# Top-k attention with a hard-swish feed-forward: the mask as a steep parametric ReLU on ScalarE, normalisation on GpSimd, and a lag of two steps

## The chip, the core and the metric

The kernel runs on one core of a Trainium2 chip. The metric is the device time of one execution in microseconds (us); the median of the runs is what is compared. The engines are TensorE (PE in the profile, its weight loads PEld), VectorE (DVE), ScalarE (ACT), GpSimd (POOL) and SyncE (SP), which issues the DMAs. Each works through its own queue in order.

## The reference

All tensors are fp32 for the kernel's computing; the two feed-forward weights arrive as 64-bit floats. For 8 batches and 8 heads, with 576 positions and a head size of 64:

```python
scores = (1.0 / np.sqrt(D)) * np.matmul(q, k.transpose(0, 1, 3, 2))
kth = np.partition(scores, -32, axis=-1)[..., -32:-31]     # 32nd largest of each row
scores = np.where(scores >= kth, scores, -1e9)
scores = scores - scores.max(-1, keepdims=True)
attn = np.exp(scores)
attn = attn / (attn.sum(-1, keepdims=True) + 1e-9)
x = np.matmul(attn, v)                  # then (B, H, S, D) -> (B*S, H*D) = (4608, 512)
h = x @ w_in                            # w_in (512, 2048)
out = (h * np.clip(h + 3.0, 0.0, 6.0) / 6.0) @ w_out       # w_out (2048, 512)
```

## The kernel before

Heads are taken in pairs (four per batch), and the 576 query rows of a pair are cut into four blocks of 128 and a rest of 64. A *unit* is one block of one pair: a full unit has 128 query rows of two heads, so 1152 scores in each partition; a rest unit has 64 rows of each head, one head in each half of the partitions, 576 scores in each partition. A batch has 20 units in five groups of four full units and one rest unit (rest last in even batches, first in odd ones): 160 units in all.

What a unit goes through:

- `scores` (L213, rest L206): TensorE multiplies into the PSUM tile `big`. `big` has one buffer, which scores, transposes of weights and transposes of inputs take in turn. ScalarE copies it to the SBUF tile `sc` (L214 and L217, rest L208).
- `top(0)` to `top(3)` (L230, L234): VectorE takes eight maxima of each row at a time and replaces them in a work tile `wk`, four times, until `m` holds the 32 largest.
- `mask` (L244, L249, L252): GpSimd compares each score with the 32nd maximum and writes 0 or -3e38 into `wk`, adds that to `sc`, and multiplies the row's maximum by minus the scale (`shift`).
- `exp` (L257): ScalarE computes exp(scale * score + shift) in place, with the row's sum in `den`; GpSimd adds 1e-9 (L262).
- `weights` (L266, L268): VectorE takes the reciprocal of `den`, ScalarE multiplies each row with it.
- `transpose` (L279, L281): TensorE transposes `sc` by blocks of 128 into `big` (nine blocks, six for a rest unit), ScalarE copies them to `eT`.
- `values` (L291, L411): TensorE multiplies with v into the PSUM tile `pv`, for two full units together or for one rest unit; ScalarE copies to `xT` or `xr`.

When four pairs of a block are there, a feed-forward is appended to a list `todo`. `piece` takes the next part from it: eight halves of an `h` tile (eight products of 128x128 each, L310; after each second one ScalarE's Relu, L318, and two pieces later VectorE's gate, L322), then eight parts of `acc` (L329), and at the end ScalarE's output copy (L339) and a DMA.

The tiles `f`, `h`, `pv` and `acc` share four PSUM buffers. In the first steps the 32 chunks of the feed-forward weights are converted from 64-bit to 32-bit by ScalarE (L106, L109), GpSimd (L107, L120) and VectorE (L115, L116); `convert_step` ends one chunk and begins another.

The order on every engine is the order in which the main loop issues the work (`manual_schedule`). A step n of this loop issues: scores of unit n+1; normalisation of unit d; `top(0)` of unit n; two pieces; `top(1)`; transposes of unit d; `top(2)`; a piece; transposes of the next pair's inputs, where due; a piece; values of unit d; `top(3)`; in every fourth step two more pieces; exp of unit n-1; mask of unit n. Here d = n - LAG with LAG = 3. In the first eight steps d = n - 1, and exp, normalisation, transposes and values of unit n-1 all stand in step n; steps 8 and 9 have no transposes.

Of the kernel before, what the change touches and what calls it, by code (L numbers as in the profile page):

```python
# [8 lines left out]
AF = mybir.ActivationFunctionType  # L9
ALU = mybir.AluOpType  # L10
F32 = mybir.dt.float32
# [3 lines left out]

TOP_K = 32
LOWEST = -3.4028234663852886e38
DROP = -3.0e38
EPS = 1.0e-9


# [5 lines left out]
def kernel(  # L27
# [9 lines left out]
    nc = tc.nc  # L37
    P = nc.NUM_PARTITIONS
    B, H, S, D = q.shape
# [8 lines left out]
    scale = 1.0 / float(D) ** 0.5  # L48

    def pool(name, bufs, **kw):  # L50
        return ctx.enter_context(tc.tile_pool(name=name, bufs=bufs, **kw))
# [1 line left out]
    consts = pool("consts", 1)  # L53
    ldpool = pool("ld", 2)
    kqpool = pool("kq", 2 * NHP)
    scpool = pool("sc", 5)
    wkpool = pool("wk", 2)
    mpool = pool("m", 4)
    etpool = pool("et", 2)
# [34 lines left out]
    def convert(dst, src):  # L94

        st = kqpool.tile([P, 2 * WC], U32, tag="kq", name="st")
        nc.sync.dma_start(st[:], src)  # L100
        words = st[:].rearrange("p (n two) -> p n two", two=2)
        lo, hi = words[:, :, 0], words[:, :, 1]
        a = gpool.tile([P, WC], F32, tag="g", name="a")
        y = gpool.tile([P, WC], F32, tag="g", name="y")
        f = ps_w.tile([P, WC], F32, tag="w", name="f")
        nc.scalar.activation(a[:], hi.bitcast(F32), AF.Abs)  # L106
        nc.gpsimd.tensor_scalar(a[:], a[:], HI_MOST, HI_LEAST, ALU.min, ALU.max)  # L107

        nc.scalar.activation(f[:], lo, AF.Copy, bias=2.0, scale=2.0**-51)  # L109
        yield  # L110

        au, yu = a[:].bitcast(U32), y[:].bitcast(U32)
        nc.vector.tensor_scalar(au, au, 3, None, ALU.logical_shift_left)  # L115
        nc.vector.scalar_tensor_tensor(  # L116
            out=yu, in0=hi, scalar=0x80000000, in1=f[:].bitcast(U32),
            op0=ALU.bitwise_and, op1=ALU.bitwise_or,
        )
        nc.gpsimd.tensor_tensor(  # L120
            dst.bitcast(I32), a[:].bitcast(I32), y[:].bitcast(I32), ALU.add
        )
# [63 lines left out]
    class Unit:  # L186
# [49 lines left out]
                    )  # L236
                    self.cur[t] = wk

        def mask(self):

            nt = self.nt
            self.shift = mpool.tile([P, 2], F32, tag="shift", name="shift")
            for t in range(nt):
                nc.gpsimd.tensor_scalar(  # L244
                    self.wk[:, t, :], self.row[t], self.m[:, t, TOP_K - 1 : TOP_K], DROP,
                    ALU.is_lt, ALU.mult,
                )
            both = self.sc[:, 0 : nt * S]
            nc.gpsimd.tensor_tensor(  # L249
                both, both, self.wk[:, 0:nt, :].rearrange("p t s -> p (t s)"), ALU.add  # L250
            )
            nc.gpsimd.tensor_scalar_mul(self.shift[:, 0:nt], self.m[:, 0:nt, 0], -scale)  # L252

        def exp(self):
            self.den = mpool.tile([P, 2], F32, tag="den", name="den")
            for t in range(self.nt):
                nc.scalar.activation(  # L257
                    self.row[t], self.row[t], AF.Exp, bias=self.shift[:, t : t + 1],
                    scale=scale, accum_out=self.den[:, t : t + 1],
                )  # L260
            d = self.den[:, 0 : self.nt]
            nc.gpsimd.tensor_scalar_add(d, d, EPS)  # L262

        def weights(self):
            d = self.den[:, 0 : self.nt]
            nc.vector.reciprocal(d, d)  # L266
            for t in range(self.nt):
                nc.scalar.activation(  # L268
                    self.row[t], self.row[t], AF.Copy, scale=self.den[:, t : t + 1]
                )  # L270

        def transpose(self):
# [10 lines left out]
        def values(self, dst):  # L283
            pr, eT = self.pair, self.eT
            for c in range(J + 1):
                for hh in range(2):
                    if self.rest:
                        rhs = eT[:, c if c < J else J + hh, hh * R : (hh + 1) * R]
                    else:
                        rhs = eT[:, c if hh == 0 or c == J else J + 1 + c, :]  # L290
                    nc.tensor.matmul(  # L291
                        dst[hh * D : (hh + 1) * D, :],
                        pr.vm[:, hh, c, :] if c < J else pr.vr[:, hh, :],
                        rhs,
                        start=(c == 0),
                        stop=(c == J),
                    )
# [51 lines left out]
    units = []  # L349
# [7 lines left out]
    NU = len(units)  # L357
# [3 lines left out]
    def piece(count=1):  # L361
        for _ in range(count):
            while todo:
                try:
                    gates.append(next(todo[0]))
                    break
                except StopIteration:
                    todo.pop(0)
            else:
                gates.append(None)  # L370
            if len(gates) > 2:
                gate = gates.pop(0)
                if gate:
                    gate()
# [4 lines left out]
    def convert_step(depth=1):  # L379

        if converting and (len(converting) > depth or not chunks):
            next(converting.pop(0), None)
        if chunks:
            c = convert(*chunks.pop(0))
            next(c)
            converting.append(c)

    EARLY = 8
    LAG = 3
    state = {}  # L390

    def values(n):
# [30 lines left out]
    def pair_at(n, first):  # L423

        b, at = divmod(n, per_batch)
        hp, odd = divmod(at - first, 3)
        return pairs[b + 1, hp] if b + 1 < B and not odd and 0 <= hp < NHP else None
# [12 lines left out]

    for n in range(NU + LAG):
        early = n < EARLY
        u = units[n] if n < NU else None
        full = not (u and u.rest)
        d = n - (1 if early else LAG)
        d = d if 0 <= d < NU and (early or d >= EARLY - 1) else None
        depth = 2 if n < 3 else 1
        if n + 1 < NU:
            units[n + 1].scores()
        if n < 2:  # L450
            pairs[0, n + 2].transpose()
        if n == 0:
            pairs[0, 3].load()
        if n in (1, 2):
            pairs[0, n + 1].load_values()
        if d is not None and not early:
            units[d].weights()
        if u:
            u.begin()
            u.top(0)  # L460
        p = pair_at(n, 6)
        if p:
            p.load()
            p.load_values()
        convert_step(depth)
        piece(2 if full else 1)
        if u:
            u.top(1)
        if d is not None:
            if early:  # L470
                units[d].exp()
            else:
                units[d].transpose()
        convert_step(depth)
        if u:
            u.top(2)
        piece()
        convert_step(depth)
        if d is not None and early:
            units[d].weights()  # L480
            units[d].transpose()
            piece()
        p = pair_at(n, 8)
        if p:
            p.transpose()
        if full and not early:
            piece()
        if d is not None:
            values(d)
        if u:  # L490
            u.top(3)
        convert_step(depth)
        if n % 4 == 3 and n > 2 * EARLY:
            piece(2)
        if not early and 1 <= n < NU + 1:
            units[n - 1].exp()
        if u:
            u.mask()
    while todo:
        piece()  # L500
    piece(2)
# [34 lines left out]
```

## Time and profile before

| | |
|---|---|
| median of three runs | 1865.07 us (1863.63 to 1865.53) |
| the profiled execution | 1863.41 us |
| its span in the profile | 1861.6 us |
| mean granted TensorE clock | 0.95 |
| busy: TensorE, VectorE, GpSimd, ScalarE | 90%, 83%, 62%, 52% of the span |

Busy times are sums over the whole span, which has three parts. In the first 200 us or so the weights are converted and TensorE is often idle. Then comes a long middle, in which the same pattern of work repeats every two batches (40 units), about 430 us. At the end, from about 1785 us, VectorE is done and TensorE works off what is left of the feed-forward. In the timeline a line gives start, duration, engine, line, operation and tiles; in brackets stands the idle time just before it and what ended that. In the list of waits the numbers are the total in us, the count and the longest. In the table of stretches, each engine's busy time stands with its count of instructions in the order TensorE, its weight loads, VectorE, ScalarE, GpSimd; the granted clock, the DMA share and GB/s follow.

### The profile page before, as it was taken

The numbers are of one execution on the slowest core, as the hardware profiler recorded it, in microseconds if no ns is written. First come the engines' busy times: TensorE is split into PE (matmuls) and PEld (weight loads), VectorE is DVE, ScalarE is ACT, GpSimd is POOL, SyncE is SP. The second block draws the span as 40 slices with busy tenths as digits, with TensorE's granted clock in tenths as the row PEclk, the third lists the DMA queues.
The fourth block names the chain that finished last, engine by engine and source line by source line (L and its number), as shares of the span: only waits on it lengthen the run. The fifth ranks groups of instructions, "written<-read, shape, count | busy, mean of one in ns | idle before, by whom it ended". The sixth has DMA issues, their size and how long they took to land.

```text
span 1861.6 us, 31024 instructions
## 1 busy us (share of the span) xinstructions
PE 1671.3 (90%) x11872; PEld 1217.5 (65%) x11872; DVE 1549.7 (83%) x3249; ACT 969.4 (52%) x1717; POOL 1157.0 (62%) x878
## 2 busy tenths in 40 slices
PE   3346799899999999899999999989999999989999
PEld 2244676567777776577677776667677767666685
DVE  5777998899988888989999888989898888989930
ACT  4553555465555555555555555555555555555540
POOL 4875676566676666666666556666666666667630
PEclk9878799899999999899999999989999999989999
DMA  6341100101001100101001100011001100000000
GB/s 190 124 122 42 43 7 7 44 20 26 7 7 45 50 7 7 45 1 45 7 6 26 45 26 7 18 34 45 7 7 26 45 26 7 6 7 7 7 7 12
DMA packets 101141, 56.54 MB, mean 30 GB/s; under 512 B 84096, under 2 KB 92288, under 8 KB 100992
## 3 DMA queue, kind: packets, MB, share of 16 engines
q1 hardware_dynamic: 100992, 54.55, 10.7%
q8 instruction: 94, 1.54, 0.4%
q14 instruction: 55, 0.45, 0.1%
HBM read 45.09 MB, written 9.44 MB: 29 GB/s over the span
## 4 chain that ended last, share of the span: by engine, by line
PE 83%; ACT 7%; POOL 6%; issue 2%; SPq 1%; DVE 1%; DMA 0%; ACTq 0%; POOLq 0%
PE h L310 28%; PE acc L329 25%; PE pv L291 10%; PE big L279 9%; PE big L213 7%; POOL wk L244 3%; POOL sc L249 2%; PE big L206 2%; ACT sc L257 2%; PE big L178 2%; ACT eT L281 2%; ACT sc L214 1%; ACT sc L268 1%; ACT a L106 1%; DMA st<-in_moe_w_in_dram 0%
## 5 line engine op out<-in xcount | busy, mean ns | idle before, releaser
L244 POOL TENSOR_SCALAR wk<-sc,m 128x576 f32<-128x576 f32 x288 | 637.1, 2220 | 14.4
L230 DVE MAX8 m<-wk 128x8 f32<-128x576 f32 x864 | 619.3, 759 | 2.8
L329 PE MATMUL acc<-w_out,g 128*128 128x512 f32 x1152 | 531.0, 601 | 0.3 <-DVE g L322 0.3
L310 PE MATMUL h<-xT,w_in 128*128 128x128 f32 x4096 | 491.6, 278 | 12.5 <-DVE y L116 10.7
L310 PEld LDWEIGHTS h<-xT,w_in 128*128 128x128 f32 x4096 | 471.6, 193 | 19.4 <-DVE y L116 11.1
L234 DVE MATCH_REPLACE8 wk<-m,wk 128x576 f32<-128x576 f32 x576 | 426.9, 754 | 0.0
L249 POOL TENSOR_TENSOR sc<-sc,wk 128x1152 f32<-128x1152 f32 (+1 forms) x160 | 381.9, 2387 | 13.4
L262 POOL TENSOR_SCALAR den<-den 128x2 f32<-128x2 f32 (+1 forms) x160 | 35.6, 223 | 547.1 <-ACT sc L257 522.6
L329 PEld LDWEIGHTS acc<-w_out,g 128*128 128x128 f32 x1152 | 206.3, 190 | 204.7 <-issue 199.7
L279 PE MATMUL big<-ident,sc 128*128 128x128 f32 x1344 | 198.4, 292 | 117.3 <-ACT sc L268 91.3
L279 PEld LDWEIGHTS big<-ident,sc 128*128 128x128 f32 x1344 | 163.6, 150 | 169.9 <-issue 109.8
L257 ACT ACTIVATE sc<-sc,shift 128x576 f32<-128x576 f32 x288 | 220.6, 769 | 50.2 <-POOL shift L252 49.8
L281 ACT COPY eT<-big 128x1152 f32<-128x1152 f32 (+1 forms) x160 | 168.8, 1055 | 135.4 <-PE big L279 134.9
L318 ACT ACTIVATE g<-h,three 128x512 f32<-128x512 f32 x144 | 99.0, 687 | 247.0 <-PE h L310 247.0
L230 DVE MAX8 m<-sc 128x8 f32<-128x576 f32 x288 | 205.0, 753 | 20.5 <-ACT sc L217 20.5
L234 DVE MATCH_REPLACE8 wk<-m,sc 128x576 f32<-128x576 f32 x288 | 213.0, 750 | 0.0
L268 ACT ACTIVATE sc<-sc,den 128x576 f32<-128x576 f32 x288 | 210.4, 777 | 2.6 <-DVE den L266 2.6
L291 PE MATMUL pv<-eT,vm 128*64 128x128 f32 (+1 forms) x2560 | 178.5, 287 | 19.3 <-ACT eT L281 19.3
L213 PE MATMUL big<-kq 64*128 64x512 f32 (+1 forms) x1024 | 178.7, 470 | 17.1 <-ACT eT L281 8.7
L291 PEld LDWEIGHTS pv<-eT,vm 128*64 128x64 f32 x2560 | 148.1, 150 | 58.1 <-ACT eT L281 38.7
L322 DVE SCALAR_TENSOR_TENSOR g<-g,h 128x512 f32<-128x512 f32 x144 | 99.0, 687 | 102.4 <-ACT g L318 102.4
L213 PEld LDWEIGHTS big<-kq 64*128 64x128 f32 x1024 | 93.9, 198 | 132.9 <-issue 96.6
(42 smaller groups left out, 999.6 us busy)
## 6 DMA issues: line engine op xcount, KB each, us to landing
kin<-in_k_dram SPq DMA_DIRECT2D x64, 128.0 KB, 2.9
qin<-in_q_dram SPq DMA_DIRECT2D x64, 128.0 KB, 2.9
st<-in_moe_w_in_dram SPq DMA_DIRECT2D x16, 512.0 KB, 4.4
vm<-in_v_dram SPq DMA_DIRECT2D x64, 128.0 KB, 2.4
st<-in_moe_w_out_dram SPq DMA_DIRECT2D x16, 512.0 KB, 3.7
out_dram<-o SPq DMA_DIRECT2D x32, 256.0 KB, 2.3
rest<-in_k_dram SPq DMA_DIRECT2D x32, 32.0 KB, 2.5
rest<-in_q_dram SPq DMA_DIRECT2D x32, 32.0 KB, 2.6
```

Source lines behind the costliest of these rows:

```text
L213: nc.tensor.matmul(banks[:, 2 * i + hh, 0 : s1 - s0], pr.qT[d, qs], pr.kT[d, s0:s1])
L230: nc.vector.max(self.m[:, t, 8 * r : 8 * r + 8], self.cur[t])
L234: nc.vector.match_replace(wk, self.m[:, t, 8 * r : 8 * r + 8], self.cur[t], LOWEST)
L244: nc.gpsimd.tensor_scalar(self.wk[:, t, :], self.row[t], self.m[:, t, TOP_K - 1 : TOP_K], DROP, ALU.is_lt, ALU.mult,)
L249: nc.gpsimd.tensor_tensor(both, both, self.wk[:, 0:nt, :].rearrange("p t s -> p (t s)"), ALU.add)
L257: nc.scalar.activation(self.row[t], self.row[t], AF.Exp, bias=self.shift[:, t : t + 1], scale=scale, accum_out=self.den[:, t : t + 1],)
L268: nc.scalar.activation(self.row[t], self.row[t], AF.Copy, scale=self.den[:, t : t + 1])
L279: nc.tensor.transpose(ps[:, i * P : (i + 1) * P], self.sc[:, c0 : c0 + P], ident[:])
L281: nc.scalar.copy(eT[:, 0:n, :].rearrange("p c q -> p (c q)"), ps[:, 0 : n * P])
L291: nc.tensor.matmul(dst[hh * D : (hh + 1) * D, :], pr.vm[:, hh, c, :] if c < J else pr.vr[:, hh, :], rhs, start=(c == 0), stop=(c == J),)
L310: nc.tensor.matmul(h[:, (f - f0) * P : (f - f0 + 1) * P], w_in[:, i, f * P : (f + 1) * P], xT[:, i, :], start=(i == 0), stop=(i == NHP - 1),)
L329: nc.tensor.matmul(acc[:], gs[f // 4][:, (f % 4) * P : (f % 4 + 1) * P], w_out[:, f, :], start=(f == 0), stop=(f == NFC - 1),)
```

## The change

`mask` is gone. In its place `exp` issues three small GpSimd operations (minus the 32nd maximum as `kth`; the scaled difference of the 32nd and the first maximum as `shift`), then on ScalarE for each row of the unit a parametric ReLU of score + kth with the slope 2^120 below zero, and then exp. What is below the threshold becomes hugely negative, and its exp zero; what is kept is the difference from the threshold, which the shift makes up for. Normalisation moves from ScalarE (a copy with a scale) to GpSimd (a multiplication by the reciprocal and by 1). `exp` of unit n stands at the end of step n, where mask stood, and normalisation of unit n-1 in step n after `top(2)` and a piece; both for all steps. LAG is 2, so step 8 alone has no transposes, and `sc` has four buffers instead of five.

```diff
-DROP = -3.0e38
+STEEP = 2.0**120
...
-    scpool = pool("sc", 5)
+    scpool = pool("sc", 4)
...
-        def mask(self):
+        def exp(self):
             nt = self.nt
-            self.shift = mpool.tile([P, 2], F32, tag="shift", name="shift")
+            kth = mpool.tile([P, 2], F32, tag="kth", name="kth")
+            shift = mpool.tile([P, 2], F32, tag="shift", name="shift")
+            self.den = mpool.tile([P, 2], F32, tag="den", name="den")
+            last = self.m[:, 0:nt, TOP_K - 1]
+            nc.gpsimd.tensor_scalar_mul(kth[:, 0:nt], last, -1.0)
+            nc.gpsimd.tensor_tensor(shift[:, 0:nt], last, self.m[:, 0:nt, 0], ALU.subtract)
+            nc.gpsimd.tensor_scalar_mul(shift[:, 0:nt], shift[:, 0:nt], scale)
             for t in range(nt):
-                nc.gpsimd.tensor_scalar(
-                    self.wk[:, t, :], self.row[t], self.m[:, t, TOP_K - 1 : TOP_K], DROP,
-                    ALU.is_lt, ALU.mult,
-                )
-            both = self.sc[:, 0 : nt * S]
-            nc.gpsimd.tensor_tensor(
-                both, both, self.wk[:, 0:nt, :].rearrange("p t s -> p (t s)"), ALU.add
-            )
-            nc.gpsimd.tensor_scalar_mul(self.shift[:, 0:nt], self.m[:, 0:nt, 0], -scale)
-        def exp(self):
...
+                nc.scalar.activation(
+                    self.row[t], self.row[t], AF.Prelu, bias=kth[:, t : t + 1], scale=1.0,
+                    alpha=STEEP,
+                )
+            for t in range(nt):
                 nc.scalar.activation(
-                    self.row[t], self.row[t], AF.Exp, bias=self.shift[:, t : t + 1],
-                    scale=scale, accum_out=self.den[:, t : t + 1],
+                    self.row[t], self.row[t], AF.Exp, bias=shift[:, t : t + 1], scale=scale,
+                    accum_out=self.den[:, t : t + 1],
                 )
...
         def weights(self):
             d = self.den[:, 0 : self.nt]
             nc.vector.reciprocal(d, d)
             for t in range(self.nt):
-                nc.scalar.activation(
-                    self.row[t], self.row[t], AF.Copy, scale=self.den[:, t : t + 1]
+                nc.gpsimd.tensor_scalar(
+                    self.row[t], self.row[t], self.den[:, t : t + 1], 1.0, ALU.mult, ALU.mult
                 )
...
-    LAG = 3
+    LAG = 2
...
-        if d is not None and not early:
-            units[d].weights()
         if u:
             u.begin()
             u.top(0)
...
         if d is not None:
-            if early:
-                units[d].exp()
-            else:
+            if not early:
                 units[d].transpose()
...
+        if 1 <= n < NU + 1:
+            units[n - 1].weights()
         if d is not None and early:
-            units[d].weights()
             units[d].transpose()
             piece()
...
-        if not early and 1 <= n < NU + 1:
-            units[n - 1].exp()
         if u:
-            u.mask()
+            u.exp()
```

More of the change, by code (lines that the diff above doesn't have):

```diff
@@ L237, in top @@
                     self.cur[t] = wk
-        def mask(self):
+        def exp(self):
             nt = self.nt
-            self.shift = mpool.tile([P, 2], F32, tag="shift", name="shift")
+            kth = mpool.tile([P, 2], F32, tag="kth", name="kth")
[5 more added lines that the diff above has]
+            nc.gpsimd.tensor_scalar_mul(shift[:, 0:nt], shift[:, 0:nt], scale)
             for t in range(nt):
-                nc.gpsimd.tensor_scalar(
-                    self.wk[:, t, :], self.row[t], self.m[:, t, TOP_K - 1 : TOP_K], DROP,
-                    ALU.is_lt, ALU.mult,
-                )
-            both = self.sc[:, 0 : nt * S]
-            nc.gpsimd.tensor_tensor(
-                both, both, self.wk[:, 0:nt, :].rearrange("p t s -> p (t s)"), ALU.add
-            )
-            nc.gpsimd.tensor_scalar_mul(self.shift[:, 0:nt], self.m[:, 0:nt, 0], -scale)
-        def exp(self):
-            self.den = mpool.tile([P, 2], F32, tag="den", name="den")
-            for t in range(self.nt):
+                nc.scalar.activation(
+                    self.row[t], self.row[t], AF.Prelu, bias=kth[:, t : t + 1], scale=1.0,
+                    alpha=STEEP,
+                )
+            for t in range(nt):
                 nc.scalar.activation(
-                    self.row[t], self.row[t], AF.Exp, bias=self.shift[:, t : t + 1],
-                    scale=scale, accum_out=self.den[:, t : t + 1],
+                    self.row[t], self.row[t], AF.Exp, bias=shift[:, t : t + 1], scale=scale,
+                    accum_out=self.den[:, t : t + 1],
                 )
-            d = self.den[:, 0 : self.nt]
+            d = self.den[:, 0:nt]
             nc.gpsimd.tensor_scalar_add(d, d, EPS)
```

## The prediction

> **What bounds the kernel now.** I began with the page: busy times and the chain that ended last.
>
> ```profile
> PE 1671.3 (90%) x11872; PEld 1217.5 (65%) x11872; DVE 1549.7 (83%) x3249; ACT 969.4 (52%) x1717; POOL 1157.0 (62%) x878
> PE 83%; ACT 7%; POOL 6%; issue 2%; SPq 1%; DVE 1%; DMA 0%; ACTq 0%; POOLq 0%
> ```
>
> TensorE carries the chain, so I asked where it isn't busy. The stretches of the span give two answers. In the first 200 us it is busy for 91 us; from 200 to 1780 for 1502 of 1580 us. The list of waits from 210 to 1780 us, TensorE alone, is short:
>
> ```profile
> PE big L279 <- ACT sc L268: 34.8, 16, 2.6
> PE pv L291 <- ACT eT L281: 16.9, 14, 1.2
> PE big L279 <- issue: 14.3, 19, 0.9
> ```
>
> L279 are the nine transposes of a unit's weights. They need the single PSUM tile `big`, thus the copy of the next scores out of it, and the normalised weights (L268). None of TensorE's waits names the mask (L244, L249). POOL's mask does hold VectorE (104.7 us at L234 from 230 to 1780), but VectorE has that time to spare there. So in the long middle the mask's 1000 us of POOL are covered; there it counts what ScalarE does between two steps of TensorE. The timeline of one step shows the race:
>
> ```profile
> 598.31 1.30 PE L213 MATMUL big<-kq 64*128 64x512 f32 x8
> 598.91 0.77 ACT L257 ACTIVATE sc<-sc,shift 128x576 f32<-128x576 f32 x1
> 599.53 2.05 PE L310 MATMUL h<-xT,w_in 128*128 128x128 f32 x16
> 600.42 0.99 ACT L214 COPY sc<-big 128x1024 f32<-128x1024 f32 x1
> 601.47 1.45 ACT L268 ACTIVATE sc<-sc,den 128x576 f32<-128x576 f32 x2
> 602.36 1.38 PE L279 MATMUL big<-ident,sc 128*128 128x128 f32 x9 [0.77 <-issue]
> ```
>
> TensorE does scores and one feed-forward piece and is there 3.28 us after 598.31; ScalarE does exp, copy and the first product and is ready after 4.05. With two pieces TensorE comes after 5.07 and waits for nothing; with none it waits 2 to 2.6 us.
>
> At the start the mask is on the path. From one reciprocal to the next:
>
> ```profile
> 62.56 0.17 DVE L266 RECIPROCAL den<-den 128x2 f32<-128x2 f32 x1 [1.77 <-POOL den L262]
> 73.31 0.61 POOL L107 TENSOR_SCALAR a<-a 128x512 f32<-128x512 f32 x1 [5.63 <-ACT a L106]
> 73.91 4.66 POOL L244 TENSOR_SCALAR wk<-sc,m 128x576 f32<-128x576 f32 x2
> 81.62 0.78 ACT L257 ACTIVATE sc<-sc,shift 128x576 f32<-128x576 f32 x1 [6.21 <-POOL shift L252]
> 83.94 0.17 DVE L266 RECIPROCAL den<-den 128x2 f32<-128x2 f32 x1 [7.49 <-POOL den L262]
> ```
>
> **Part 1, the start (mask off POOL, products on POOL).** Out of the loop go the mask, 4.66 + 2.61 + 0.24 with gaps 7.4 us, and ScalarE's first product, 0.8. In come three small POOL operations at 0.23 (row L252), 0.7; two Prelus, for which I take L268's pair, 0.67 from start to start, 1.3; the first product on POOL; and a queue. `exp` now stands at the end of a step, so POOL's `den` stands ahead of three chunks of weight conversion, and the products stand behind those. The third clamp (L107) needs ScalarE to have done the scores' copy (1.2) and three pairs L106/L109 (1.2 each): 5.5 us after `den` the products start. The product's price is the large unknown; POOL has no such multiplication in this trace. Nearest rows:
>
> ```profile
> L107 POOL TENSOR_SCALAR a<-a 128x512 f32<-128x512 f32 x32 | 20.2, 633 | 44.1 <-ACT a L106 43.6
> L244 POOL TENSOR_SCALAR wk<-sc,m 128x576 f32<-128x576 f32 x288 | 637.1, 2220 | 14.4
> ```
>
> Both do two operations on one input. L107 scaled to 576 columns gives 0.71 us; L244, with a pointer scalar as in the change but a comparison, 2.22. I take 0.71, because two plain arithmetic operations are L107's form, and keep 2.22 for the range. The Trainium skill (GPSIMD Engine Reference, 3.1) says that a body of at most two operations runs at 1.03 cycles an element, and that data-dependent branching costs about 12; by that estimate the product is about 0.5 us plus dispatch and the start would gain some 2 us more, while L244 with 2220 ns shows that it isn't so for every two-operation form.
>
> Per loop: -7.4 - 0.8 + 0.7 + 1.3 + 0.7 + 5.5 = 0. The loops alone give nothing, and what is gained lies elsewhere. The first exp no longer waits for the first mask (43.4 us now; small operations after the clamp at 35.1, so 36.7): -6.7. The three stalls of 3.6, 4.1 and 6.4 us in which VectorE's L116 waits for POOL behind a mask (at 113, 130 and 150 us) shorten; POOL is blocked by `den` instead, so I count half, -7. Between the early steps and the late ones the order has two steps without transposes now (lag 3), one after (lag 2), and the transposes of unit 7 at 192.7 wait 8.9 us behind the next unit's exp, which waits for its mask; that goes, but copies and scores that were in the gap then take time: -4. Against it, TensorE reaches the feed-forward with one scores (1.3) and one pair transpose (1.5) not yet done: +2.8. Sum -15. Bounds: 0 (POOL product 2.22 in each of some eight loops) to -30 (the stalls go entirely and the gap too).
>
> **Part 2, the middle.** ScalarE's sum per unit is the same: two products (1.45) go, two Prelus come. But their place changes. The products stood behind the scores' copy and only the first had to be done; both Prelus stand ahead of the copy, and the transposes wait for its end. From the start of `exp`: now 1.51 (exp) + 1.05 (copy) + 0.78 + 0.11 = 3.45; after, 1.34 + 1.51 + 1.17 + 0.11 = 4.13. So +0.68 us per full unit wherever TensorE is already waiting. Lag 2 also changes which step the values (L291) end in. From the order of the built instructions, over the repeating 40 units (430 us): of the steps between scores and transposes four have no piece now and five after; seven have one piece now, six after, and in five of these the values come just before, so that the copy L411 (0.39 with its latency) stands ahead of the Prelus.
>
> One piece: ready after 0.39 + 4.13 = 4.52 against 3.25, idle 1.27 (four times), 1.48 behind the output copy, 0.9 where the next unit is a rest unit (its copy is 0.63): 7.5 us. Now the trace has 0.67, 0.93, 0.77, 0.86, 0.50, 0.50: 4.2. No piece: now 2.55 and three times 2.05, 8.7; after 3.2, 1.4 (exp of a rest unit, 1.6, ends before the scores do) and three times 2.2: 11.2. Copies L281 with nothing beside them: five now, six after, at 1.21: 6.1 and 7.3. Together 19.0 and 26.0 us: +7 per 430 us. Three whole rounds and the last 20 units (+5): +26.
>
> The clock adds to it. The step with no piece at 844.9 us (idle 2.05, then 1.21 before the values) shows in the stretches as
>
> ```profile
> 840.00:850.00 10.00, 6.74 (x45) 4.51 (x45) 10.00 (x24) 6.06 (x10) 6.72 (x4) 0.82 0.45 114
> 850.00:860.00 10.00, 10.00 (x84) 8.85 (x81) 9.82 (x21) 5.18 (x10) 6.56 (x6) 0.84 0.39 93
> ```
>
> PEclk is the third number from the end: (0.18 + 0.16) x 10 = 3.4 us lost, 0.9 of it idle already counted: 2.5 for the new step of this kind, four times, +10. The Trainium skill (TensorE: Matmul & The Clock Gate, HAM oscillation) names idle gaps over about 3.4 us as what throttles; by it neither gap would cost clock and the middle would be +26. The row shows 2.05 and 1.21 us enough, so I keep +36.
>
> What is hidden: VectorE's reciprocal moves behind `top(2)`; behind it stand gates and `top(3)`. It waits for `den`, 3.4 us after ScalarE starts `exp`; VectorE then has 1.4 us to its step's end, and TensorE's step takes 7 to 14, so VectorE stays ahead (five units take it 47 us, from 197.3 to 246.9 less a stall of 2.5, and TensorE 54, an eighth of 430). If that lead went, ScalarE's Prelu would wait for VectorE's last maximum, with scores' copy, Relus and TensorE's transposes queued behind: up to 2 us in each step with no piece, 40 us in all. POOL after: three small operations, two products, `den`, 2.5 us per unit; nobody waits for that in the middle. A fourth buffer of `sc` suffices: the row is transposed two steps later. SP's queue and the DMAs are in the same order, one step apart at most.
>
> **Sum.** The profiled execution took 1863.4 (span 1861.6); the median shown is 1.7 above it. 1863.4 - 15 + 36 = 1884.4, with the 1.7 about 1886. The case's own range, with clock from 0 to +15 and the start from -25 to -5: 1866 to 1902.
>
> **Rivals.** A, faster: the start alone counts. If the transposes in steps with one and no piece wait no longer than now, the middle stays and the time is 1850. It decides at the 0.68 us between products behind and Prelus ahead of the copy: for it, ScalarE is 52% busy and before the copy often idle for 2 to 3 us, in which a Prelu could run early; against it, the 598 us timeline, in which ScalarE has no gap. B: POOL's product costs 2.22, the start gains nothing: 1863.4 + 36 + 1.7 = 1901. Against it L107. C: the idle of 1.3 to 1.5 us in the one-piece steps throttles the clock too, 6 x 3.6 times 1.7 us (the loss at 470 us): +37, 1923. Against it, 0.9 us now costs nothing (clock 1.00 around 602); the threshold lies between 0.9 and 3.3. D: start and middle cancel, 1865. That Prelu lies in another table than Exp and ScalarE reloads all the time: the built order has one table load, as now, so I give it nothing.
>
> **Numbers.** My case 0.50, A 0.22, B 0.13, C 0.07, D 0.08. The range 1848 to 1912 leaves out C and the lower half of A. About 0.2% (4 us) is what a measurement can tell from no change. Faster 0.22, same 0.08, slower 0.70.
>
> **What would show it.** Right: Prelu near 0.77 us, POOL's product near 0.7; TensorE's waits at the transposes name the scores' copy (L215, L218), 1.2 to 1.5 us in steps with one piece; the first piece of the second feed-forward near 195 us instead of 210.5; clock dips at five places per round. Wrong: Prelu's wait for POOL or VectorE in every step (VectorE leads less than I think), products of 2 us, or total TensorE idle after 230 us at or under today's 75 us.

## The result and the profile after

The changed kernel took 1877.74 us (median of four runs, 1876.84 to 1879.55) against 1865.30 of the kernel before beside it (1863.63 to 1865.76). The ratio is 1.007, 95% interval 1.0052 to 1.0087: slower by 0.7%, where 1886 was forecast. The profiled execution took 1877.58 us, its span grew from 1861.6 to 1875.8. Some line numbers shift: Prelu is L251, exp L256, `den` L261, the reciprocal L265, the product L267, the transposes L278, the copy of `eT` L280, the copies of the scores L215 and L218.

Busy times and the chain that ended last, from the page of the changed kernel:

```profile
PE 1672.3 (89%) x11872; PEld 1228.7 (66%) x11872; DVE 1550.3 (83%) x3249; ACT 964.2 (51%) x1717; POOL 409.0 (22%) x1038
PE 82%; ACT 10%; issue 3%; POOL 3%; DVE 1%; SPq 1%; DMA 1%; ACTq 0%
```

GpSimd lost two thirds of its work (1157.0 to 409.0 us) and the kernel became slower. ScalarE does as much as before, and its share of the chain rose from 7 to 10%. The costs of the new operations, from the costliest groups with shapes apart (busy time and mean ns of one behind the first bar):

```profile
L267 POOL TENSOR_SCALAR sc<-sc,den 128x576 f32<-128x576 f32 x288 | 212.5, 747 | 368.3 <-DVE den L265 362.9 <-PE big L278 2.4 <-PE h L309 1.6
L251 ACT ACTIVATE sc<-sc,kth 128x576 f32<-128x576 f32 x288 | 208.7, 769 | 34.3 <-POOL kth L247 34.3
L247 POOL TENSOR_SCALAR kth<-m 128x2 f32<-128x2 f32 x128 | 29.1, 227 | 89.2 <-DVE m L231 88.8
```

All three are near the forecast (0.71, 0.77 and 0.23 us). TensorE's waits in the middle, from 210 to 1790 us (total, count, longest):

```profile
PE big L278 <- ACT sc L218: 44.4, 20, 3.2
PE big L278 <- POOL den L261: 23.4, 18, 1.4
PE pv L290 <- ACT eT L280: 21.7, 18, 1.2
PE big L214 <- ACT kq L185: 5.1, 4, 1.3
PE big L278 <- ACT sc L209: 3.7, 4, 0.9
```

The first two and the last are the transposes, 34.8 + 14.3 us before and 71.5 after (L209 is the scores' copy of a rest unit). The second names POOL's `den`, but misleadingly, as one step in the timeline shows:

```profile
599.63 1.30 PE L214 MATMUL big<-kq 64*128 64x512 f32 x8
599.75 0.37 ACT L410 COPY xT<-pv 128x256 f32<-128x256 f32 x1 [1.66 <-PE pv L290]
600.01 1.44 ACT L251 ACTIVATE sc<-sc,kth 128x576 f32<-128x576 f32 x2
...
600.86 2.05 PE L309 MATMUL h<-xT,w_in 128*128 128x128 f32 x16
601.36 0.76 ACT L256 ACTIVATE sc<-sc,shift 128x576 f32<-128x576 f32 x1
...
602.12 0.76 ACT L256 ACTIVATE sc<-sc,shift 128x576 f32<-128x576 f32 x1
...
602.87 0.99 ACT L215 COPY sc<-big 128x1024 f32<-128x1024 f32 x1
603.05 0.22 POOL L261 TENSOR_SCALAR den<-den 128x2 f32<-128x2 f32 x1 [7.68 <-ACT sc L256]
...
603.76 0.27 ACT L218 COPY sc<-big 128x128 f32<-128x128 f32 x1
...
604.13 1.18 PE L278 MATMUL big<-ident,sc 128*128 128x128 f32 x9 [1.22 <-POOL den L261]
```

`den` was done at 603.27; what ended at 604.03, just before the transposes, is the second half of the scores' copy, on ScalarE. The queue there is copy of `xT`, two Prelus, two exps, copy: ready 4.50 us after the scores began, where TensorE came after 3.28. The row that the prediction worked out as 4.52 is this one.

At the start, one loop:

```profile
55.14 0.28 POOL L247 TENSOR_SCALAR kth<-m 128x2 f32<-128x2 f32 x1
...
55.45 1.44 ACT L251 ACTIVATE sc<-sc,kth 128x576 f32<-128x576 f32 x2 [0.56 <-POOL kth L247]
...
58.48 0.22 POOL L261 TENSOR_SCALAR den<-den 128x2 f32<-128x2 f32 x1 [2.61 <-ACT sc L256]
58.78 1.39 POOL L121 TENSOR_TENSOR w_in<-a,y 128x512 int32<-128x512 int32 x1
...
64.06 0.61 POOL L108 TENSOR_SCALAR a<-a 128x512 f32<-128x512 f32 x1
...
64.77 1.47 POOL L267 TENSOR_SCALAR sc<-sc,den 128x576 f32<-128x576 f32 x2
...
65.57 2.18 PE L278 MATMUL big<-ident,sc 128*128 128x128 f32 x9 [9.33 <-POOL sc L267]
```

The exp chain begins 4.9 us earlier than in the loop before (55.45 for 60.32), but between `den` and the products POOL works off three additions (L121) and three clamps (L108) of the conversion: the products start 6.3 us after `den`.

**Ledger of the span.** Since the order repeats, the transposes of one unit in each 40 serve as a mark; in the kernel before they stand at 359.86 and 1649.94 us, after at 346.81 and 1663.03, three rounds apart. The first piece of the second feed-forward came at 191.97 instead of 210.51 (-18.5), with 2.5 us of other work not yet done: start -16. From there to the first mark +3; three rounds of 438.7 instead of 430.0, +26; the rest +1. Sum +14.

### The profile page after: what moved, and what is told of

Read it like the earlier page. It is cut to its first block, busy times and chain, and to the rows that moved or that the text cites. A ratio compares the mean times of both kernels' runs of the same rounds, so it can differ in the third digit from the quotient of the medians.

```text
span 1875.8 us, 30943 instructions
## 1 busy us (share of the span) xinstructions
PE 1672.3 (89%) x11872; PEld 1228.7 (66%) x11872; DVE 1550.3 (83%) x3249; ACT 964.2 (51%) x1717; POOL 409.0 (22%) x1038
## 4 chain that ended last, share of the span: by engine, by line
PE 82%; ACT 10%; issue 3%; POOL 3%; DVE 1%; SPq 1%; DMA 1%; ACTq 0%
PE h L309 27%; PE acc L328 25%; PE pv L290 11%; PE big L278 9%; PE big L214 6%; ACT sc L256 3%; ACT eT L280 2%; ACT sc L251 2%; PE big L207 2%; PE big L179 2%; ACT sc L215 1%; POOL a L108 1%; POOL w_in L121 1%; ACT o L338 1%; POOL w_out L121 1%
## 5 line engine op out<-in xcount | busy, mean ns | idle before, releaser
L278 PE MATMUL big<-ident,sc 128*128 128x128 f32 x1344 | 189.8, 289 | 122.5 <-ACT sc L218 49.2
L267 POOL TENSOR_SCALAR sc<-sc,den 128x576 f32<-128x576 f32 x288 | 212.5, 747 | 368.3 <-DVE den L265 362.9
L278 PEld LDWEIGHTS big<-ident,sc 128*128 128x128 f32 x1344 | 163.2, 150 | 163.5 <-POOL den L261 78.4
L280 ACT COPY eT<-big 128x1152 f32<-128x1152 f32 (+1 forms) x160 | 169.1, 1057 | 183.3 <-PE big L278 183.3
L251 ACT ACTIVATE sc<-sc,kth 128x576 f32<-128x576 f32 x288 | 208.7, 769 | 34.3 <-POOL kth L247 34.3
L261 POOL TENSOR_SCALAR den<-den 128x2 f32<-128x2 f32 (+1 forms) x160 | 34.9, 218 | 868.1 <-ACT sc L256 868.1
L256 ACT ACTIVATE sc<-sc,shift 128x576 f32<-128x576 f32 x288 | 219.4, 763 | 3.3 <-ACT sc L251 0.4
L290 PE MATMUL pv<-eT,vm 128*64 128x128 f32 (+1 forms) x2560 | 188.6, 298 | 25.4 <-ACT eT L280 25.4
L290 PEld LDWEIGHTS pv<-eT,vm 128*64 128x64 f32 x2560 | 157.1, 156 | 62.9 <-ACT eT L280 32.0
L214 PE MATMUL big<-kq 64*128 64x512 f32 (+1 forms) x1024 | 179.8, 472 | 20.1 <-ACT kq L185 11.7
L410 ACT COPY xT<-pv 128x256 f32<-128x256 f32 x64 | 23.8, 373 | 232.5 <-PE pv L290 232.5
```

The costliest lines, as they stand in the source:

```text
L214: nc.tensor.matmul(banks[:, 2 * i + hh, 0 : s1 - s0], pr.qT[d, qs], pr.kT[d, s0:s1])
L251: nc.scalar.activation(self.row[t], self.row[t], AF.Prelu, bias=kth[:, t : t + 1], scale=1.0, alpha=STEEP,)
L256: nc.scalar.activation(self.row[t], self.row[t], AF.Exp, bias=shift[:, t : t + 1], scale=scale, accum_out=self.den[:, t : t + 1],)
L267: nc.gpsimd.tensor_scalar(self.row[t], self.row[t], self.den[:, t : t + 1], 1.0, ALU.mult, ALU.mult)
L278: nc.tensor.transpose(ps[:, i * P : (i + 1) * P], self.sc[:, c0 : c0 + P], ident[:])
L280: nc.scalar.copy(eT[:, 0:n, :].rearrange("p c q -> p (c q)"), ps[:, 0 : n * P])
```

## The experiments

Every kernel was timed beside the kernel before, on the same chip; the ratio is to that, with its 95% interval. A round is the mean of the three rounds of 40 units between the first mark and the last; the other columns are means over the same rounds. Idle is TensorE's, busy what its 2968 matmuls took. In the traces the granted clock is either 1.00 or 0.50, and "clock" is the part of busy that this costs, taken as half of the busy time at 0.50. Busy less clock is 397.7 to 398.8 us in all rows but the first and the third, where it is 400.7.

| kernel | median us | ratio | round | idle | busy | clock |
|---|---|---|---|---|---|---|
| before | 1865.3 | 1 | 430.0 | 19.0 | 411.1 | 10.4 |
| changed | 1877.7 | 1.007 (1.0052 to 1.0087) | 438.7 | 27.1 | 411.7 | 13.3 |
| start alone | 1856.8 | 0.9954 (0.994 to 0.9969) | 430.0 | 19.0 | 411.1 | 10.4 |
| changed, lag 3 | 1862.6 | 0.9983 (0.9973 to 0.9993) | 432.3 | 23.1 | 409.2 | 11.2 |
| changed, products on ScalarE | 1873.6 | 1.0048 (1.0031 to 1.0065) | 440.3 | 29.5 | 410.8 | 12.0 |
| changed, products doubled | 1893.5 | 1.0148 (1.0133 to 1.0163) | 438.8 | 28.2 | 410.6 | 11.9 |
| changed, no Prelu in the middle | 1809.7 | 0.9701 (0.9684 to 0.9717) | 421.0 | 15.9 | 405.1 | 6.7 |
| both behind the copy | 1832.4 | 0.9825 (0.981 to 0.9839) | 426.4 | 19.3 | 407.1 | 9.2 |
| exp behind the copy | 1807.2 | 0.9688 (0.9674 to 0.9703) | 420.4 | 16.2 | 404.2 | 6.5 |
| exp behind the copy, lag 3 | 1818.3 | 0.9747 (0.9732 to 0.9761) | 420.3 | 13.7 | 406.5 | 8.8 |
| before, exp behind the copy | 1824.2 | 0.9775 (0.9758 to 0.9791) | 419.4 | 13.2 | 406.1 | 8.3 |
| exp behind the copy, early products on ScalarE | 1795.4 | 0.9623 (0.9606 to 0.964) | 419.5 | 16.5 | 403.0 | 5.0 |
| exp behind the copy, early products sooner | 1796.1 | 0.9626 (0.9611 to 0.964) | 420.6 | 16.1 | 404.5 | 6.6 |

The theory: in the middle the time is set by what ScalarE has queued ahead of the scores' copy; at the start, by the queues between exp and transposes. Rivals: the Prelu as such, lag 2, POOL's product.

**Exp behind the copy.** `exp` is cut in two; its second half is issued a step later.

```diff
-            shift = mpool.tile([P, 2], F32, tag="shift", name="shift")
+            shift = self.shift = mpool.tile([P, 2], F32, tag="shift", name="shift")
...
                     alpha=STEEP,
                 )
+        def exp2(self):
+            nt, shift = self.nt, self.shift
             for t in range(nt):
                 nc.scalar.activation(
                     self.row[t], self.row[t], AF.Exp, bias=shift[:, t : t + 1], scale=scale,
...
             units[n + 1].scores()
+        if EARLY < n <= NU:
+            units[n - 1].exp2()
...
             u.exp()
+            if n < EARLY:
+                u.exp2()
```

> Only the place of exp's second half is changed: the Prelus stay at the end of step n, the exps (and den) of unit n are issued in step n+1 behind the copy of the next scores, from step 9 on; the first eight steps as in the changed kernel. Theory (what costs the middle is the length of ScalarE's chain ahead of the scores' copy): without the two exps (1.52 us in the trace after) the copy ends 3.0 us after the scores start instead of 4.5, TensorE comes after 3.28 with one piece, so the six waits of 0.9 to 1.4 us in one-piece steps go (-7.5 per round of 40 units), and those with no piece fall from 11.1 to about 7.2: -11.4 per round, 3.65 rounds, 1877.7 - 41 = 1837 (1830 to 1850). Rival 1 (Prelu as such is the price, wherever exp stands): 1870 to 1880. Rival 2 (the exps behind the copy delay the copy of eT, and VectorE's reciprocal comes later): 1850 to 1865.

1807.2 us, below the expected range. The timeline of the step that was shown above, now (exp is L259, the transposes L281, the copy of `eT` L283, the piece L312):

```profile
583.73 1.30 PE L214 MATMUL big<-kq 64*128 64x512 f32 x8
...
584.11 1.44 ACT L251 ACTIVATE sc<-sc,kth 128x576 f32<-128x576 f32 x2
...
584.96 2.05 PE L312 MATMUL h<-xT,w_in 128*128 128x128 f32 x16
585.46 1.00 ACT L215 COPY sc<-big 128x1024 f32<-128x1024 f32 x1
586.35 0.28 ACT L218 COPY sc<-big 128x128 f32<-128x128 f32 x1
586.51 0.79 ACT L259 ACTIVATE sc<-sc,shift 128x576 f32<-128x576 f32 x1
...
586.84 1.15 PE L281 MATMUL big<-ident,sc 128*128 128x128 f32 x9
...
588.03 1.12 ACT L283 COPY eT<-big 128x1152 f32<-128x1152 f32 x1
```

The copy ends 2.90 us after the scores begin, the transposes follow the piece with no wait, and exp runs beside them. Idle per round fell by 10.9 us, near what was expected (11.4). But the round fell by 18.3: the same 2968 matmuls took 7.5 us less, 6.8 of it in the clock column. The expectation left out that idle which goes takes clock losses with it.

**No Prelu in the middle.** Without the mask from unit 8 on, so that the output is not the reference's there; nothing else changed.

```diff
-            for t in range(nt):
+            for t in range(nt if self.early else 0):
                 nc.scalar.activation(
                     self.row[t], self.row[t], AF.Prelu, bias=kth[:, t : t + 1], scale=1.0,
...
+            u.early = n < EARLY
             u.exp()
```

> Leaves out the mask: no Prelu from unit 8 on, so exp runs over all scores and the output is not the reference's there; all else as in the changed kernel. It prices the Prelus in the middle. Theory (chain ahead of the scores' copy): 1.34 us less ahead of the copy, ready after 3.2 us against 3.28 with one piece, so one-piece waits vanish (-7.5 per round) and no-piece waits fall from 11.1 to about 7.4: -11 per round, 1877.7 - 41 = 1837 (1830 to 1848), the same as with the exps moved. Rival (the middle's loss comes from lag 2 and the new order, not from the Prelus): 1865 or more.

1809.7 us and 15.9 us idle a round, nearly the same as with the Prelus kept and the exps moved (16.2). So a Prelu costs the middle nothing in ScalarE's time as such; its place ahead of the copy, with exp there too, costs 17.7 us a round. The size was again underestimated, because only the idle was counted: the clock column fell from 13.3 to 6.7 us.

**Both behind the copy.**

```diff
         if n + 1 < NU:
             units[n + 1].scores()
+        if EARLY < n <= NU:
+            units[n - 1].exp()
...
-            u.exp()
+            if n < EARLY:
+                u.exp()
```

> Prelus and exps of unit n both issued in step n+1 behind the copy of the next scores, from step 9 on. Theory: the copy follows the scores at once, one-piece waits vanish and no-piece waits fall from 11.1 to about 6.5 per round; but 2.95 us of ScalarE then stand between the scores' copy and the copy of eT, so eT's waits in steps with no piece grow from 7.3 to about 10 per round: 27.1 becomes 17.9, 1845 (1838 to 1858), slower than with the exps alone moved. Rival (ScalarE's chain ahead of the copy is not what counts): 1878.

1832.4 us: slower than with the exps alone moved, as the theory has it, but below the expected range. The new wait is in the list of TensorE's waits for one round (768.7 to 1195 us), where the next scores wait up to 2.6 us for the copy of `eT`, which now stands behind 3 us of Prelus and exps:

```profile
PE big L278 <- ACT sc L218: 6.6, 5, 1.3
PE pv L290 <- ACT eT L280: 5.3, 4, 1.4
PE big L214 <- ACT eT L280: 4.4, 5, 2.6
```

**The start alone.** The kernel before, with the changed `exp` and `weights` added as `exp_e` and `weights_e`, for units 0 to 6.

```diff
-            if early:
-                units[d].exp()
-            else:
+            if not early:
                 units[d].transpose()
...
-            units[d].weights()
+            units[d].weights_e()
             units[d].transpose()
...
-            u.mask()
+            if n < EARLY - 1:
+                u.exp_e()
+            else:
+                u.mask()
```

> The start alone: units 0 to 6 take the changed kernel's exp (Prelu) and POOL product at the changed places; from unit 7 on everything as before (mask on POOL, products on ScalarE, lag 3). Theory: the middle is as before, the start gains what the changed kernel's start gains (16 us) less the part that lag 2 gives (about 4): 1865.3 - 12 = 1853 (1847 to 1860). Rival (the start's gain comes from lag 2, in which one step without transposes goes): 1862 to 1866.

1856.8 us. The round is that of the kernel before, the first mark comes 7.5 us earlier. So of the 16 us that the change gains at the start about half lies in mask and products, half in lag 2, which I had put at 4.

**Changed, lag 3.**

```diff
-    scpool = pool("sc", 4)
+    scpool = pool("sc", 5)
...
-    LAG = 2
+    LAG = 3
```

> The changed kernel with LAG 3 and five buffers of sc instead of 2 and four; Prelus and products as in the change. From the order of the built instructions a round of 40 units then has four steps with no piece instead of five, and eight with one piece, none of them behind the values. Theory (chain ahead of the copy and the order of lag 2 both count): one-piece waits 8 x 0.88 = 7.0, no-piece about 9, eT 6.1: 22 instead of 27.1 per round, with a clock dip less -7 per round, 3.65 rounds -25; the start loses one step without transposes, about +7: 1877.7 - 18 = 1860 (1852 to 1870). Rival (lag 2 costs nothing in the middle, the Prelus are all): 1877.7 + 7 = 1885.

1862.6 us. Of the 8.7 us that a round lost, 6.4 go with lag 2 and its order. What is left against the kernel before, 2.3, is 4.1 us more idle and 0.8 more of clock, less 2.7 that the transposes gained (below). The shares are not independent: with the exps out of the way lag 2 costs nothing (420.4 and 420.3 in the table).

**Changed, products on ScalarE.**

```diff
-                nc.gpsimd.tensor_scalar(
-                    self.row[t], self.row[t], self.den[:, t : t + 1], 1.0, ALU.mult, ALU.mult
+                nc.scalar.activation(
+                    self.row[t], self.row[t], AF.Copy, scale=self.den[:, t : t + 1]
                 )
```

> The products back on ScalarE (a copy with a scale), at the place and in the order of the change; Prelus, lag 2 and four buffers as in the change. Theory (the products are off the path in the middle, and what counts there is the Prelus' place): ScalarE gets 1.45 us more per unit, but after the copy of the scores, where it is idle half the time; the Prelus come later in some steps only; at the start 0.8 us per loop on ScalarE in place of 0.75 on POOL behind its conversions: 1880 (1874 to 1890). Rival (a product on ScalarE, waiting for VectorE's reciprocal, holds the copies of eT and xT and the Relus in each step): 1900 or more.

1873.6 us, 4 less than with POOL's products and just below the expected range: the middle was as expected, the start was not. In the middle it costs 1.6 us a round, near what was expected, although ScalarE is 62% busy instead of 51%. The start, expected even, is 12.6 us faster at the first mark. After the same `den` the product starts 4.25 us later on ScalarE (56.97, 61.22) and 6.3 later on POOL. Moving the products to GpSimd is a loss at the start and a small gain in the middle.

**Changed, products doubled.**

```diff
+    ones = consts.tile([P, 2], F32, tag="ones", name="ones")
+    nc.gpsimd.memset(ones[:], 1.0)
...
+                nc.gpsimd.tensor_scalar(
+                    self.row[t], self.row[t], ones[:, t : t + 1], 1.0, ALU.mult, ALU.mult
+                )
```

> The changed kernel with each POOL product done twice (the second by ones), so POOL's share of a unit grows by 1.5 us. Theory (POOL's product is on the path at the start only): seven loops x 1.5 = +10 at most, part of it beside the wait for the scores, middle 0: 1886 (1880 to 1890). Rival 1 (POOL's product is hidden at the start too): 1878. Rival 2 (POOL's products are waited for in the middle as well): +1.5 in each of the 10 waiting steps of a round, 1920 or more.

1893.5 us: +15.8, more than expected, of which 11.7 by the first mark, nothing in the three rounds and the rest after them, where its cause was not looked for. POOL's product is on the path at the start and off it in the middle. As an estimate by the same slope, a product of 2.22 us (rival B) would have cost 15.8 x 1.47 / 0.75 = 31 us.

**Exp behind the copy, lag 3.** The first experiment with LAG 3 and five buffers of `sc`.

> The exps moved behind the copy of the next scores (Prelus stay ahead), with LAG 3 and five buffers of sc. Theory: one-piece waits stay at zero, four steps with no piece instead of five (1.7 + 1.2 us less per round, and what clock that dip costs), 3.65 rounds -14, the start +7: 1807.2 - 7 = 1800 (1794 to 1812). Rival (with lag 3 the start's loss outweighs it): 1810 to 1815.

1818.3 us, 11 more than with lag 2: a miss. Idle fell by 2.5 us a round, near the 2.9 expected, but the matmuls took 2.3 us more, all of it in the clock column, so the round stayed as it was. Where two steps with no piece follow each other, ScalarE's Prelus now wait for `kth`, and that for VectorE's last maximum:

```profile
762.79 0.23 POOL L247 TENSOR_SCALAR kth<-m 128x2 f32<-128x2 f32 x1 [0.55 <-DVE m L231]
763.06 1.44 ACT L251 ACTIVATE sc<-sc,kth 128x576 f32<-128x576 f32 x2 [2.13 <-POOL kth L247]
764.40 0.99 ACT L215 COPY sc<-big 128x1024 f32<-128x1024 f32 x1
```

The start lost the 8 us of the second step without transposes (first piece at 200.44 for 192.45). Of the 11 us, 4.7 remain at the first mark and 5.9 stand behind the last one, where the clock alone, priced as in the table, costs 6.3 us more; neither was forecast.

**Exp behind the copy, with the early products made sooner, in two ways.** The 13 us that POOL's product costs at the start can be the engine's or its queue's. One kernel gives the products of units 0 to 6 to ScalarE; the other leaves them on POOL, but issues them after `top(1)`.

```diff
-        def weights(self):
+        def weights(self, act=False):
...
             for t in range(self.nt):
+                if act:
+                    nc.scalar.activation(
+                        self.row[t], self.row[t], AF.Copy, scale=self.den[:, t : t + 1]
+                    )
+                    continue
...
-            units[n - 1].weights()
+            units[n - 1].weights(early)
```

> Exps moved behind the copy of the next scores, lag 2, and the products of units 0 to 6 on ScalarE (as in the run with all products there), of the later ones on POOL. Theory (at the start the products on POOL stand behind conversion chunks; on ScalarE the same transposes came 13 us earlier, at 170.3 instead of 183.2): 1807.2 - 13 = 1794 (1790 to 1800). Rival (what the start gains is given back, since VectorE, 86% busy, then bounds the middle): 1803 to 1808.

```diff
             if not early:
                 units[d].transpose()
+            else:
+                units[n - 1].weights()
...
-        if 1 <= n < NU + 1:
+        if EARLY <= n < NU + 1:
             units[n - 1].weights()
```

> As the kernel with the exps moved, all products on POOL, but in the first eight steps reciprocal and products are issued after top(1) instead of after top(2) and a piece, so that one or two conversion chunks fewer (clamp and addition, 1.9 us each) stand ahead of them on POOL. Theory (the queue's order, not the engine, makes POOL's product late): about 2.5 us per loop on six loops, 1807.2 - 13 = 1794 (1789 to 1801), as with the products on ScalarE. Rival (the product on POOL is late because POOL itself is full of conversions): 1805 to 1810.

1795.4 and 1796.1 us: the same within their intervals, 12 and 11 below the kernel with the exps moved. It is the queue. POOL's stretch of one loop in the second kernel shows one addition and one clamp ahead of the products instead of three of each:

```profile
56.89 0.22 POOL L264 TENSOR_SCALAR den<-den 128x2 f32<-128x2 f32 x1 [2.61 <-ACT sc L259]
57.18 1.27 POOL L121 TENSOR_TENSOR w_in<-a,y 128x512 int32<-128x512 int32 x1
58.54 0.67 POOL L108 TENSOR_SCALAR a<-a 128x512 f32<-128x512 f32 x1
59.30 1.47 POOL L270 TENSOR_SCALAR sc<-sc,den 128x576 f32<-128x576 f32 x2
```

These two versions beat both kernels; against the kernel before they gain 3.7 to 3.8%.

**The kernel before, with ScalarE's order alone changed.** Mask on GpSimd, products on ScalarE, lag 3 and start as they were; GpSimd's `den` goes with the exps and VectorE's reciprocal with the products.

```diff
-        if d is not None and not early:
-            units[d].weights()
+        if 0 <= n - 2 < NU and n - 2 >= EARLY - 1:
+            units[n - 2].exp()
...
-        if not early and 1 <= n < NU + 1:
-            units[n - 1].exp()
+        if 0 <= n - 2 < NU and n - 2 >= EARLY - 1:
+            units[n - 2].weights()
```

> The kernel before (mask on GpSimd, products on ScalarE, lag 3, its start as it was), with only ScalarE's order in the middle changed: exp of a unit behind the copy of the next scores one step later, its two products at the end of that step, so that only they (1.45 us, as the two Prelus) stand ahead of the next copy. Theory (what sets the middle is how much ScalarE has ahead of the scores' copy, whoever applies the mask): a round of 40 units takes 420.3 us as in the two kernels with the exps moved, against 430.0: 1865.5 - 3.65 x 9.7 = 1830 (1824 to 1842). Rival (the Prelu is what makes the gain possible, since GpSimd's mask of 7.4 us per unit then ends too late for exp or holds VectorE): 1855 or more.

1824.2 us, the round 419.4. The middle of the best kernels is had without Prelu, GpSimd's products or lag 2. GpSimd's mask of 7.4 us per unit stays hidden: of TensorE's waits from 230 to 1740 us one, of 1.9 us, names it.

## Why the prediction was right, and where it was not

- **Bound.** Confirmed: the middle goes by TensorE and ScalarE's queue ahead of the scores' copy, and 748 us off GpSimd bought nothing there.
- **Chain, 4.13 us, ready after 4.52.** Measured 4.50. The steps with one piece wait 0.9 to 1.4, those with no piece 1.3, 2.2 (three times) and 3.2, as worked out. The queue behind the inputs' transposes was not foreseen: a step that ends in them lets the next scores wait 1.27 us for the copy L185. Idle per round is 27.1 for 26.0 forecast, and +8.1 for +7.
- **Clock, +10.** Right in size. TensorE's busy time in the stretches at clock 0.50 of the three rounds, before and after:

```profile
sum 81.76, PE 62.12; mean PE 6.21
sum 101.06, PE 79.57; mean PE 6.12
```

  Half of it is lost, 31.1 and 39.8 us: +8.7, where 2.5 a round made 7.5. The places were not as forecast: such stretches stand at four places a round for three before, not at five, and the longest, at the two steps with no piece in a row, last 17.1 us before and 10.2 to 17.1 after.
- **A term that the sum does not have: shorter transposes.** Over three rounds TensorE's busy time rose by only 1.8 us (1233.2 to 1235.0), since the transposes took 142.8 before and 137.0 after, and without their share of the clock's loss 136.3 and 129.9. In the kernel before they begin after the first product, and the second half waits for the second:

```profile
602.98 0.53 PEld L279 LDWEIGHTS big<-ident,sc 128*128 128x128 f32 x5 [0.23 <-ACT sc L268]
```

  The nine transposes took 1.38 us there; in the step shown above, with both products long done, 1.18. So the 26 us of three rounds are 24.3 of idle and 8.7 of clock, less 6.9, of which 6.5 are the transposes.
- **Last 20 units, +5.** Measured +3 ahead of the first mark and +1 behind the last. The middle as a whole is +30, not +36; without the shorter transposes it would have been near the forecast.
- **Start, -15.** Measured -16, but the terms are not those of the forecast, and that the sum fits is luck. The first exp's chain, with its Prelus, did begin 6.4 us sooner (43.4 to 37.0; forecast -6.7), yet the first transposes came 2.5 us later, released by GpSimd's product:

```profile
47.98 2.15 PE L279 MATMUL big<-ident,sc 128*128 128x128 f32 x9 [10.20 <-ACT sc L268]
50.44 2.18 PE L278 MATMUL big<-ident,sc 128*128 128x128 f32 x9 [7.18 <-POOL sc L267]
```

  Up to the fifth unit's transposes nothing is gained (120.1 and 119.9 us); at the seventh it is 7.5 us (163.4 and 155.9), at the eighth, where lag 2 saves a step without transposes, 16.6 (193.4 and 176.8). Lag 2's share is thus near 8 for the 4 given. VectorE's stalls at L116 (L117 after), from 0 to 200 us, fell by 5.4 us (forecast -7), but its waits for GpSimd's clamp grew by 5.9; two lines before, two after:

```profile
DVE y L116 <- POOL w_out L120: 14.0, 3, 6.3
DVE a L115 <- POOL a L107: 2.2, 1, 2.2
DVE y L117 <- POOL w_out L121: 8.6, 3, 3.5
DVE a L116 <- POOL a L108: 8.1, 7, 2.7
```

  What gave the 7.5 us between the fifth and the seventh unit is open. Products start 6.3 us after `den` for 5.5.
- **Rivals.** A fails: the waits at the transposes grew. Its ground, that ScalarE is half idle, is true but of no use, since the queue is in order. B fails: 747 ns. C fails: steps with one piece and 1.2 to 1.4 us of idle show a clock of 1.00 (at 550, 604 and 659 us), and the last section shows why. D fails in size: -16 and +30.

## What to carry to other kernels

Where one engine waits for an instruction of another, count what stands in the other's queue ahead of that one instruction; here 1.5 us a unit moved from ahead of it to behind it were worth more than 748 us taken off a third engine. Price a wait with the clock that it costs, and reprice the neighbouring waits too. Before an operation is moved to an idle engine, look at what its queue holds at the place where it will be issued: order, not speed, made GpSimd's product late.

## What was not expected of the hardware

Idle is worth more than its length: taking 10.9 us of waits out of a round shortened the same 2968 matmuls by 7.5 us. The granted clock falls after quite short gaps, but not each time. In all 13 traces a stretch at clock 0.50 lasts 3.41 us or a multiple of it (but for one that the end of the program cuts off), and every 3.41 us of it cost up to 1.7 us. In the kernel with the exps behind the copy, idle of 1.52 us and, after the transposes, 1.21 us (at 861 to 865 us) is followed by such a stretch, and the same pair of gaps at 811 to 815 us is not. Cut into stretches of 3.41 us that line up with those at 0.50, the trace shows the difference, the second pair first (TensorE's busy time stands behind the length, the clock third from the end):

```profile
809.78:813.19 3.41, 1.89 (x16) 1.00 0.35 109
813.19:816.60 3.41, 2.20 (x25) 1.00 0.74 174
860.98:864.39 3.41, 1.29 (x12) 1.00 0.21 79
864.39:867.80 3.41, 2.80 (x26) 0.50 0.00 0
```

At 811 the two gaps fall into two stretches, 1.52 and 1.21 us of idle; at 861 one stretch holds 2.12 us of them, and the next is at half clock. The same cut through all 13 traces from 230 to 1740 us leaves no exception: each of the 142 full-clock stretches with more than 1.75 us idle (1.76 to 3.26) is followed by one at 0.50, and none of the 5266 with 1.75 us or less is. What counts is how much idle falls into one such stretch, about half of it, and not the length of a gap; so the price of a wait depends on where it happens to lie.

The Trainium skill (TensorE: Matmul & The Clock Gate, What's actually happening) describes a gate that halves the rate for free-running windows of about 3.4 us, and these traces agree: one such grid holds through the middle of each of them. The same page's rule that gaps over about 3.4 us are what throttles (HAM oscillation) is too lenient for this case: in the pair that counts no gap was over 1.52 us.
